# Rebuilding the opening of a linear-attention and MoE kernel: one-bank products for the first 512 tokens, weights cut at column 256, squares redistributed

## The chip, the cores and the metric

One Trainium2 chip, one core. The metric is the device time of one execution in microseconds (us), read on the core. The "clock" of an execution is the mean TensorE clock that its record shows, as a share of full speed.

## The reference, cut to what matters

```python
# q, k, v: [8 batches, 8 heads, 576, 64] f32
q_s = softmax(q, over the 64 dims)
k_s = softmax(k, over the 576 positions)
kv  = einsum('bhsd,bhse->bhde', k_s, v)
x   = einsum('bhsd,bhde->bhse', q_s, kv) -> [4608 tokens, 512]
h   = x @ w_in                       # 512 x 2048
g   = h + sin(alpha * h)**2 / alpha
out = g @ w_out                      # 2048 x 512
```

The 4608 tokens are nine tiles of 512. A batch has 576 tokens, so tile 0 is all of batch 0 but its last 64 tokens. The 2048 hidden columns are 16 "units" of 128. A unit of a tile is four first-layer products, a sine on ScalarE, a square on one of three engines, and a combine (`g`) on VectorE, which frees the unit's PSUM buffer. Then 64 second-layer products follow.

## The kernel before

```python
def load_win(c0, c1):                       # first-layer weights, f32 -> bf16 on the way
    n = slice(c0 * 512, c1 * 512)
    for x in range(2):                      # two halves of the partitions
        nc.gpsimd.dma_start(out=win[64 * x:64 * x + 64, :, n], in_=win_v[x][:, :, n])
...
# opening: batch 0
warm_up(14)                                 # dummy products
norm_q(0, [GP, V])
for c0, c1 in ((0, 1), (1, 2), (2, 4)):     # columns 0-511, 512-1023, 1024-2047
    load_win(c0, c1)
for c in range(3):
    load_wout(c)
cast_v0(0, ACT_CP); cast_v0(1, DVE_CP)
q_transpose(0, 0, ps_s, ACT_CP); q_transpose(0, 1, ps_s, DVE_CP)
cast_v0(2, DVE_CP)
for ii in range(2):
    kv_mm(0, ii, ps_s, split=True); kv_norm(0, ii, ii + 1)
for ii in range(2):                         # all 576 tokens, two-bank products
    attn_out(0, ii, 0, ps_s, (ACT_CP, DVE_CP)[ii])
    attn_out(0, ii, 1, ps_s, (ACT_CP, DVE_CP)[ii])
    warm_up((1, 4)[ii])
...
# tile 0: which engine squares which unit (P GpSimd, A ScalarE, D VectorE)
late = {3: ("q", q, 1, True), 6: ("k", k, 1, False), 8: ("v", v, 1, True)}
for ni in range(nN):
    h_slot(0, ni, "PAPDPAPADPAPPDAP"[ni], lag, lent)
    flush(lag, 1)
    if ni in late:
        ...                                 # loads of batch 1, issued by GpSimd
    if ni == 11:
        load_wout(3)
...
cast_v(1, [GP, GP])
accs = [ps_h.tile([128, dm], F32, name="hp", tag="h") for _ in range(4)]   # of the 4 buffers of ps_h
os = o_quad(0, accs, ...)                   # the 64 second-layer products of tile 0
```

`load_wout` issues a quarter of the second-layer weights, also from GpSimd. The issues: each occupies GpSimd's queue for 0.64 to 0.83 us, and its squares stand in that queue too.

The softmax here doesn't subtract the row's maximum and nothing guards it: scores larger than these inputs give would overflow.

## Time and profile before

| | before |
|---|---|
| median of 3 executions | 296.62 us (296.46 to 296.97) |
| span of the profiled execution | 294.8 us |
| first product of tile 0 | 17.64 us |
| second-layer products before the wait for the accumulators | 9 |
| TensorE resumes after that wait | 34.12 us |
| first product of tile 1 | 49.75 us |

The timelines that carry the argument are in the prediction below. A line of a timeline gives the start and the length of a run of like instructions, then engine, line, operation, "output<-input" and the count; in brackets how long the engine was idle just before, and who ended that. Two more lines of before: the clock row of the page (tenths of full speed in 40 slices), and, from TensorE's timeline, the first product that needs batch 2's q, which a DMA transposes.

```profile
PEclk9999999999999999999999999999999999999999
```

```profile
78.62 0.38 PE L198 MATMUL xp<-qT,kbd 128*128 128x256 bf16 x2 [1.06 <-DMA qT<-qn]
```

### The profile page before, as it was taken

Reading aid. Unit: us, or ns where it says so; the run is one execution under the profiler, and the core shown is the slowest. Engines: PE = TensorE matmul, PEld = TensorE weight load, DVE = VectorE, ACT = ScalarE, POOL = GpSimd, SP = SyncE. Lnnn points to the kernel's source line nnn. Section 1 sums busy time; section 2 is a strip of 40 time slices with the busy share of each in tenths; the row PEclk is TensorE's granted clock in tenths of the full one; section 3 lists DMA queues with packets and bytes.
Section 4 is the critical chain, followed back from the end, with each engine's and each line's share of the span. In section 5 each row is a group of like instructions: output and inputs, shape, how many; then the busy total and the mean of one; then the engine's idle time right before and its main releaser. Section 6 shows DMA issues by size and latency. Waiting matters only on the chain.

```text
span 294.8 us, 4250 instructions
## 1 busy us (share of the span) xinstructions
PE 279.5 (95%) x1576; PEld 132.4 (45%) x1576; DVE 185.9 (63%) x270; ACT 228.1 (77%) x320; POOL 84.6 (29%) x73
## 2 busy tenths in 40 slices
PE   2999999999799999999999999999999999999994
PEld 1544445444344444444444444444444444444443
DVE  3758955789638857865687568756875455555421
ACT  4679855999578899879987999799977777777500
POOL 0939590575665536000700061005000000000000
PEclk9999999999999999999999999999999999999999
DMA  7999989955859986108921794112411111111143
GB/s 261 281 191 207 366 234 364 390 189 165 183 85 323 392 282 139 28 21 290 330 50 36 235 337 98 36 39 60 91 38 36 36 36 38 36 36 37 46 99 72
DMA packets 35221, 45.77 MB, mean 155 GB/s; under 512 B 15856, under 2 KB 19712, under 8 KB 35200
## 3 DMA queue, kind: packets, MB, share of 16 engines
q1 hardware_dynamic: 29600, 34.09, 40.6%
q0 software_dynamic: 5408, 11.27, 14.9%
q8 instruction: 12, 0.20, 0.3%
q10 hardware_dynamic: 192, 0.14, 0.2%
q14 instruction: 9, 0.07, 0.1%
HBM read 36.71 MB, written 9.44 MB: 157 GB/s over the span
## 4 chain that ended last, share of the span: by engine, by line
PE 75%; DVE 9%; ACT 5%; POOL 3%; DMA 3%; issue 2%; ACTq 0%; SPq 0%
PE op L235 31%; PE hp L215 30%; PE hp L235 4%; DVE g L231 3%; PE xp L198 3%; PE warm L279 2%; POOL s L225 2%; DVE xT L201 2%; ACT s L221 2%; PE kvp L154 2%; DMA qT<-qn 2%; DMA st_q<-in_q_dram 1%; DVE o L241 1%; ACT xT L201 1%; PE op L468 1%
## 5 line engine op out<-in xcount | busy, mean ns | idle before, releaser
L231 DVE SCALAR_TENSOR_TENSOR g<-s,inva_sb,hp 128x512 bf16<-128x512 f32 x130 | 95.3, 746 | 65.1 <-ACT s L223 52.3
L215 PE MATMUL hp<-xT,win 128*128 128x512 bf16 x520 | 129.7, 379 | 0.3
L235 PE MATMUL op<-wout,g 128*128 128x512 bf16 x496 | 123.8, 379 | 0.0
L221 ACT ACTIVATE s<-hp,alpha_sb 128x512 f32<-128x512 f32 x130 | 87.8, 682 | 27.0 <-PE hp L215 23.0
L215 PEld LDWEIGHTS <-win 128*128 128x128 bf16 x576 | 56.1, 98 | 68.3 <-issue 2.3
L235 PEld LDWEIGHTS <-g 128*128 128x128 bf16 x560 | 54.0, 98 | 61.9 <-issue 1.0
L223 ACT ACTIVATE s<-s 128x512 f32<-128x512 f32 x112 | 70.5, 629 | 3.6
L144 POOL TENSOR_TENSOR qn<-qe,qs 128x2304 bf16<-128x2304 bf16 (+1 forms) x8 | 26.6, 3328 | 85.2 <-DVE qs L143 79.5
L225 POOL TENSOR_TENSOR s<-s 128x512 f32<-128x512 f32 x27 | 28.4, 1058 | 25.9 <-ACT s L221 25.7
L241 DVE COPY o<-op 128x512 f32<-128x512 f32 (+1 forms) x33 | 21.9, 663 | 14.2 <-PE op L235 11.8
L142 DVE TENSOR_REDUCE qs<-qe 128x18 f32<-128x1152 bf16 (+1 forms) x11 | 20.7, 1880 | 13.1 <-ACT qe L114 13.0
L114 ACT ACTIVATE qe<-st_q 128x1152 bf16<-128x1152 f32 x16 | 17.8, 1155 | 2.8 <-DMA st_q<-in_q_dram 2.7
L114 ACT ACTIVATE ke<-st_k 128x1152 bf16<-128x1152 f32 x16 | 17.7, 1150 | 2.5 <-DMA st_k<-in_k_dram 2.5
L128 POOL CAST vb<-st_v 128x1152 bf16<-128x1152 f32 x14 | 16.5, 1210 | 7.9 <-DMA st_v<-in_v_dram 7.9
L201 DVE CAST xT<-xp 128x512 bf16<-128x512 f32 (+1 forms) x22 | 16.5, 753 | 2.8 <-PE xp L198 2.7
L198 PE MATMUL xp<-qT,kbd 128*128 128x256 bf16 (+1 forms) x64 | 12.4, 285 | 4.2 <-ACT xT L201 1.8
L235 PE MATMUL hp<-wout,g 128*128 128x512 bf16 x64 | 15.1, 379 | 0.4 <-DVE g L231 0.3
L198 PEld LDWEIGHTS <-kbd 128*128 128x128 bf16 x64 | 6.0, 97 | 12.9 <-issue 5.7
L201 ACT CAST xT<-xp 128x512 bf16<-128x512 f32 (+1 forms) x10 | 6.3, 638 | 7.0 <-PE xp L198 6.9
L279 PE MATMUL warm<-qe,identb 128*128 128x512 bf16 x19 | 7.5, 562 | 2.8 <-ACT qe L114 2.8
L154 PE MATMUL kvp<-vb,ke 64*128 64x130 bf16 x288 | 9.8, 216 | 0.4 <-ACT qT L183 0.3
L114 ACT ACT_TABLE_LOAD x7 | 9.0, 1283 | 1.3 <-PEq L484 1.2
(51 smaller groups left out, 112.2 us busy)
## 6 DMA issues: line engine op xcount, KB each, us to landing
out_dram<-o SPq DMA_DIRECT2D x70, 128.0 KB, 2.4
st_q<-in_q_dram SPq DMA_DIRECT2D x5, 1152.0 KB, 6.3
st_k<-in_k_dram SPq DMA_DIRECT2D x5, 1152.0 KB, 8.7
st_v<-in_v_dram SPq DMA_DIRECT2D x5, 1152.0 KB, 10.7
st_k<-in_k_dram POOLq DMA_DIRECT2D x2, 1152.0 KB, 10.8
wout<-in_moe_w_out_dram POOLq DMA_DIRECT2D x4, 512.0 KB, 14.4
st_q<-in_q_dram SPq DMA_DIRECT2D x2, 576.0 KB, 4.6
st_k<-in_k_dram SPq DMA_DIRECT2D x2, 576.0 KB, 6.6
```

The costliest lines, as they stand in the source:

```text
L114: nc.scalar.activation(dst[:, :, ii * 128:(ii + 1) * 128].rearrange("p j (x d) -> p x j d", x=2), src[:, ii::2], AX.Exp)
L142: nc.vector.tensor_reduce(part, src, axis=AXL.X, op=ALU.add)
L144: engs[h].tensor_tensor(dst, src, part.unsqueeze(3).to_broadcast([128, J, w, D]), op=ALU.mult)
L198: nc.tensor.matmul(xp[:, e, 0:n], kt[:, e, ii], qT[:, j0:j1, ii, e * 64:(e + 1) * 64], start=True, stop=True)
L201: eng(xT[:, 2 * ii:2 * ii + 2, c0:c0 + n], xp[:, :, 0:n])
L215: nc.tensor.matmul(hp, win[:, ki, ni * 128:(ni + 1) * 128], xT[:, ki, t * MF:(t + 1) * MF], start=(ki == 0), stop=(ki == 3))
L221: nc.scalar.activation(s, hp, AX.Sin, scale=alpha_sb[:, ni:ni + 1])
L223: nc.scalar.activation(s, s, AX.Square)
L225: nc.gpsimd.tensor_tensor(s, s, s, op=ALU.mult)
L231: nc.vector.scalar_tensor_tensor(G[t][:, ni], in0=s, scalar=inva_sb[:, ni:ni + 1], in1=hp, op0=ALU.mult, op1=ALU.add)
L235: nc.tensor.matmul(acc, G[t][:, ni, j * 128:(j + 1) * 128], wout[:, ni, :], start=(ni == 0), stop=(ni == nN - 1))
L241: eng(o[:, cols], acc)
```

## The change

The intent: give tile 0 its 512 tokens sooner. Batch 0's attention makes four one-bank chunks of 512 tokens (the other 64 tokens follow later), tile 0's first two units start on half of the model dims, and the warm-ups (dummy products) fall from 19 to 10. With this came three things: the first weights are cut at columns 256 and 1024, with the fourth transfer issued after a cast of v on GpSimd; the string of squares and the places of GpSimd's issues are new; batch 1's v is cast by ScalarE and VectorE. The normalised q and its transpose also exchange two axes, through the whole run.

```diff
-    def load_win(c0, c1):
-        n = slice(c0 * 512, c1 * 512)
-        for x in range(2):
+    def load_win(c0, c1, xs):
+        n = slice(c0, c1)
+        for x in xs:
... (qn and qT: axis ii moved ahead of j; copies of qT split in two)
-        warm_up(14)
+    warm_up(9)
-        for c0, c1 in ((0, 1), (1, 2), (2, 4)):
-            load_win(c0, c1)
-        for c in range(3):
-            load_wout(c)
+    load_win(0, 256, (0,))
+    load_win(0, 256, (1,))
+    load_win(256, 1024, (0,))
... (transposes of q in parts)
-        cast_v0(2, DVE_CP)
+    cast_v0(2, GP_CP)
+    load_win(256, 1024, (1,))
+    load_win(1024, 2048, (0, 1))
+    for c in range(2):
+        load_wout(c)
...
+    for c in range(4):
+        xp = ps_h.tile([128, MF], F32, name="hp", tag="h")
+        attn_chunk(0, c, 0, 8, xp)
+        (ACT_CP, DVE_CP)[c % 2](xT[:, c, 0:MF], xp)
...
-        late = {3: ("q", q, 1, True), 6: ("k", k, 1, False), 8: ("v", v, 1, True)}
+        late = {3: ("q", q, 1, True), 7: ("k", k, 1, False), 9: ("v", v, 1, True)}
+        for ni in range(2):
+            mm_h(0, ni, lent, 0, 2)
-            h_slot(0, ni, "PAPDPAPADPAPPDAP"[ni], lag, lent)
+            h_slot(0, ni, "DAPPAPPDPAPPDPAP"[ni], lag, lent)
-            if ni == 11:
-                load_wout(3)
+            if ni in (5, 12):
+                load_wout(2 if ni == 5 else 3)
-        cast_v(1, [GP, GP])
+        cast_v(1, [ACT_CP, DVE_CP])
... (the 64 tokens left over: four small products and one copy among the second-layer products)
```

## The prediction

> **What bounds the kernel now.** I read the first page (busy shares, then the chain by line), then each engine's timeline of the first 50 us, because the change ends there: later it only reorders the axes of the normalised q and its transpose, and splits some instructions.
>
> ```profile
> PE 279.5 (95%) x1576; PEld 132.4 (45%) x1576; DVE 185.9 (63%) x270; ACT 228.1 (77%) x320; POOL 84.6 (29%) x73
> ...
> PE 75%; DVE 9%; ACT 5%; POOL 3%; DMA 3%; issue 2%; ACTq 0%; SPq 0%
> ```
>
> TensorE is busy for 95% and carries 75% of the chain that ends last. Only an opening that lets its dense work start earlier, and keeps it dense, can win. TensorE's timeline from there:
>
> ```profile
> 6.07 6.13 PE L279 MATMUL warm<-qe,identb 128*128 128x512 bf16 x14 [2.82 <-ACT qe L114]
> 12.00 1.22 PE L182 MATMUL tp<-identb,qn 128*128 128x128 bf16 x18
> 13.15 1.46 PE L154 MATMUL kvp<-vb,ke 64*128 64x130 bf16 x36
> ...
> 17.64 1.89 PE L215 MATMUL hp<-xT,win 128*128 128x512 bf16 x8
> ...
> 29.74 1.89 PE L215 MATMUL hh<-xT,win 128*128 128x512 bf16 x8
> 31.47 2.38 PE L235 MATMUL hp<-wout,g 128*128 128x512 bf16 x9
> 34.12 7.71 PE L235 MATMUL hp<-wout,g 128*128 128x512 bf16 x35 [0.28 <-DVE g L231]
> 41.68 0.83 PE L182 MATMUL tp<-identb,qn 128*128 128x128 bf16 x12
> ...
> 44.04 1.20 PE L154 MATMUL kvp<-vb,ke 64*128 64x130 bf16 x36 [0.33 <-ACT qT L183]
> ...
> 49.75 0.59 PE L215 MATMUL hp<-xT,win 128*128 128x512 bf16 x2
> ```
>
> The first real products start at 17.64 us. Tile 0's 64 of them last to 31.47: 13.83 us, 216 ns each, no gap. Nine products of the second layer follow and there is a short wait (0.28 us) for VectorE's result; at 44.04 another (0.33 us) for ScalarE's copy of q transposed. So tile 0 has almost no slack in TensorE: 2 us won at 17.64 would be a full 2 us, if the others keep up. GpSimd's timeline says that they may not:
>
> ```profile
> 19.48 1.03 POOL L225 TENSOR_TENSOR s<-s 128x512 f32<-128x512 f32 x1 [3.43 <-ACT s L221]
> 21.57 1.04 POOL L225 TENSOR_TENSOR s<-s 128x512 f32<-128x512 f32 x1 [1.06 <-ACT s L221]
> 22.55 1.49 POOL L91 DMA_DIRECT2D st_q<-in_q_dram  x2
> 24.05 2.06 POOL L225 TENSOR_TENSOR s<-s 128x512 f32<-128x512 f32 x2
> 26.03 0.80 POOL L93 DMA_DIRECT2D st_k<-in_k_dram  x1
> 26.82 1.42 POOL L91 DMA_DIRECT2D st_v<-in_v_dram  x2
> 28.25 2.15 POOL L225 TENSOR_TENSOR s<-s 128x512 f32<-128x512 f32 x2
> 30.34 0.79 POOL L107 DMA_DIRECT2D wout<-in_moe_w_out_dram  x1
> 31.14 1.05 POOL L225 TENSOR_TENSOR s<-s 128x512 f32<-128x512 f32 x1
> 32.84 1.04 POOL L225 TENSOR_TENSOR s<-s 128x512 f32<-128x512 f32 x1 [0.65 <-ACT s L221]
> ```
>
> From 21.57 to 32.19 GpSimd has no gap: squares of 1.04 us and DMA issues of 0.7 to 0.8 us stand in one queue. It is 29% busy over the run, but in tile 0 it is a second bound.
>
> **What the Trainium skill says.** "DMA: Bandwidth & Descriptors", section "SWDGE vs HWDGE vs iDMA": a DMA that casts can only be issued by GpSimd, which computes its descriptors in software. The trace agrees: each issue occupies GpSimd for 0.64 to 0.83 us. Same page, "Why small descriptors are slow (HBM only)": each packet has a fixed cost. From the DMA view, 705 packets of 0.98 KB (written size) in 14 to 18 us, at a busy share of 1.12 on 16 engines, are 102 ns each; 476 of 1.79 KB in 18 to 22 us, at 1.14, are 153 ns. That is about 40 ns plus 63 ns per KB: it agrees. "TensorE: Matmul & The Clock Gate", part 1: cold products of 512 columns take 427 ns and warm ones 216. Here the 14 warm-ups take 438 ns each, the later products 216, though the clock row reads full: it agrees. "ScalarE: Activation LUTs", "What ACT_TABLE_LOAD costs": 1.283 us; the trace has 1.28.
>
> **The change, part by part: the opening.** Loads of q, k, v are untouched: ScalarE's exponentials still end at 10.54, v's first half lands at 10.90, its last piece about 12.5 (issued near 4.2, 8.3 to land). Warm-ups fall from 14 to 9 (-2.2 us of TensorE), so the transposes of half 0 go right after GpSimd's q (ends 9.99), those of half 1 after VectorE's (11.21), and are done about 12.3 instead of 13.2. ScalarE casts v to 12.07, so k-v products run 12.3 to 13.1 for half 0; GpSimd casts the last piece (512 columns, about 0.55) to 13.05; half 1 ends near 13.7. VectorE normalises, 0.18 + 0.59 each with small gaps: 13.1 to 13.9 and 13.9 to 14.7 (before 14.06 to 15.70). The four chunks are then evacuated alternately: ScalarE 14.35 to 14.95, VectorE 14.75 to 15.45, ScalarE 15.1 to 15.7, VectorE to 16.1. The split groups let products start on the first two chunks, so I place the first at about 15.5 instead of 17.64: 2.1 us. ScalarE loads its sine table to 17.0, first sine at about 17.2 instead of 18.71: 1.5 us.
>
> **The weights' arrival.** In before, columns 0 to 511 of the first weights land at 14.5 and 15.6, columns 512 to 1023 at about 18.4 and 19.1. Now 0 to 255 come first, then 256 to 1023 as one transfer per half. By the packet line, 512 packets of 0.5 KB take 512 x 72 / 16 = 2.3 us and 512 of 1.5 KB 512 x 135 / 16 = 4.3 us; 1024 packets of 1 KB, as now, 1024 x 103 / 16 = 6.6. So the first 1024 columns are complete when they are now, 18.5 to 19.3. Units 0 and 1 can run early (8 products, done by 17.2), but unit 2 needs column 256 and so waits to some 18.7. In before unit 2 started at 19.37. What is left of 2.1 us on TensorE is 0.7 (0 to 1.2).
>
> **The squares.** The string of before gives GpSimd 8 squares and 4.5 us of issues, and one square is done by 20.5. The new one gives it units 2, 3, 5, 6, 8, 10, 11, 13, 15: nine, none early, and a third block of second-layer weights is now issued inside the stage. The sum is 9 x 1.04 + 1.49 + 0.79 + 0.80 + 1.43 + 0.79 = 14.7 us. It can't start before unit 2's sine. If the weights were no limit, that ends at 17.2 + 0.65 + 0.65 + 0.63 (the square of unit 1 on ScalarE) + 0.65 = 19.8; with them at 18.7, 18.7 + 0.86 + 0.2 + 0.65 = 20.4. So GpSimd ends at 34.5 to 35.1, against 33.88 now. Unit 13's square ends 1.04 before, its combine 0.7 later: 34.1 to 34.8. The fourth accumulator takes that unit's PSUM slot, so TensorE resumes dense work there, against 34.12 now. The first two accumulators wait likewise for units 10 and 11 (about 32.5 to 33; now 31.4), so 8 products are done by then, not 9: 0.2 more. Stage result: +0.3 to +1.0.
>
> **Batch 1.** Its v cast moves from GpSimd (2.9 us, done 42.6) to ScalarE and VectorE. v lands at 39.6 and 40.7 whatever the order, since DMA is full until then and the bytes ahead are the same; the casts end about 41.6. But the k-v products at 44.04 wait for ScalarE's copy of the transposed q, not for v, so this saves nothing unless TensorE arrives earlier. Four small products for the 64 tokens left over add 0.15 us, two copies of 768 for one of 1536 about 0.1. Sum: +0.5 to +1.3, middle +0.9. After this TensorE's stages shift as a whole.
>
> **Rivals.** (1) The gain carries through: GpSimd is not what releases the accumulators, or the weights land by 17.5. That the squares were shifted towards GpSimd speaks for it: whoever retuned them should have seen room there. Products start 2.1 us earlier, v's casts allow it at 41.6 instead of 44.04: 294.5 to 295.5. Against it is the gapless queue above. (2) Weights late: small packets run worse than my line, or the cast between the issues leaves a hole. Unit 2 starts at 19.5 to 20, everything moves by a further 0.8: 298.5 to 299. (3) Fewer warm-ups leave TensorE cold: tile 0's first products at 427 ns, up to 1.5 us. Against it: TensorE stays busy from 6.07 to 13.7, and those first products have slack before unit 2. About nothing.
>
> **Range and chances.** The working alone says 297.5. I give rival 1 about a third, because a retuned string suggests a measured benefit that I can't see, and pull the number to 297.0. Range 294.4 to 298.9: rival 1 in full is its low end, rival 2 the high. Two per cent is 5.9 us; the whole span ahead of the first product changes by 2.1, so beyond 2% either way is very unlikely: faster 0.02, same 0.965, slower 0.015.
>
> **What would show it.** First product near 15.5; a hole in TensorE of 1 to 2 us ahead of unit 2, ended by the weights' DMA; GpSimd gapless from about 20.4 to 35; second-layer products starting near 32.5 and resuming after 34.1, VectorE named as releaser; k-v products of batch 1 at 44.5 to 45.3, after ScalarE's copy; tile 1's first product at 50.2 to 51. I am wrong if GpSimd's queue ends before 33 or tile 1 starts before 49.

## The result, and the profile after

The median of four executions is 300.60 us (300.16 to 301.24), of before in the same rounds 296.76 (296.46 to 296.97): a ratio of 1.0132, 95% interval 1.0109 to 1.0155. That is within 2%, but above the predicted range of 294.4 to 298.9. Ratios here are the mean time of one kernel's fast runs over that of the other's fast runs of the same rounds, so not quite the ratio of the medians.

The page after: TensorE's share fell, DMA's share of the chain rose from 3% to 7%, and two slices of the clock row read 8.

```profile
PE 278.6 (93%) x1567; PEld 131.3 (44%) x1567; DVE 186.4 (62%) x272; ACT 228.6 (76%) x322; POOL 84.8 (28%) x78
...
PEclk9988999999999999999999999999999999999999
...
PE 72%; DVE 8%; DMA 7%; POOL 4%; ACT 4%; issue 2%; SPq 1%; ACTq 0%
```

TensorE's timeline after, to be held against the one in the prediction:

```profile
14.28 0.40 PE L154 MATMUL kvp<-vb,ke 64*128 64x130 bf16 x8 [0.71 <-POOL vb L307]
...
16.03 1.95 PE L234 MATMUL hp<-xT,win 128*128 128x512 bf16 x8
21.26 3.26 PE L234 MATMUL hh<-xT,win 128*128 128x512 bf16 x8 [3.28 <-DMA win<-in_moe_w_in_dram]
24.36 3.62 PE L234 MATMUL hp<-xT,win 128*128 128x512 bf16 x16
...
36.28 0.38 PE L254 MATMUL hp<-wout,g 128*128 128x512 bf16 x1 [0.58 <-DVE g L250]
37.71 4.26 PE L254 MATMUL hp<-wout,g 128*128 128x512 bf16 x19 [1.05 <-DVE g L250]
...
49.51 1.20 PE L154 MATMUL kvp<-vb,ke 64*128 64x130 bf16 x36 [0.38 <-DVE qT L187]
...
55.22 3.62 PE L234 MATMUL hp<-xT,win 128*128 128x512 bf16 x16
...
83.42 0.38 PE L206 MATMUL xp<-qT,kbd 128*128 128x256 bf16 x2 [0.39 <-DMA qT<-qn]
```

The first eight products start at 16.03, 1.6 us earlier than before. Then TensorE stands for 3.28 us until the weights of columns 256 to 1023 land. The next eight products (units 2 and 3) last from 21.26 to 24.36, 3.10 us, where eight at 216 ns are 1.73. In the second layer one product, not nine, is done before the accumulators stop it, and tile 1 starts at 55.22 instead of 49.75. (The first eight products go by turns to accumulators 1 and 2, so the second product already needs accumulator 2. An accumulator takes the PSUM buffer of one of the units 10 to 13 and is free when that unit is combined.)

The windows view of TensorE shows why those eight were slow. Columns: stretch in us, its length, TensorE busy (instructions), granted clock, DMA share, GB/s.

```profile
20.50:21.00 0.50, 0.00 (x0) 0.66 1.12 185
21.00:21.50 0.50, 0.24 (x1) 0.50 0.99 147
...
24.00:24.50 0.50, 0.50 (x3) 0.93 1.14 190
```

The clock stands at 0.50 from 20.66 to 24.07 (0.66 and 0.93 are averages over half a microsecond, in which it changes): TensorE ran at half speed just as the weights came.

GpSimd's timeline after:

```profile
13.61 0.62 POOL L307 CAST vb<-st_v 128x512 bf16<-128x512 f32 x1 [1.68 <-DMA st_v<-in_v_dram]
14.17 1.85 POOL L104 DMA_DIRECT2D win<-in_moe_w_in_dram  x3
...
23.93 1.03 POOL L244 TENSOR_TENSOR s<-s 128x512 f32<-128x512 f32 x1 [6.41 <-ACT s L240]
...
34.40 2.04 POOL L244 TENSOR_TENSOR s<-s 128x512 f32<-128x512 f32 x2
...
38.52 1.04 POOL L244 TENSOR_TENSOR s<-s 128x512 f32<-128x512 f32 x1 [0.28 <-ACT s L240]
```

The queue of squares and issues now begins at 23.93 (before: a square at 19.48, and gapless from 21.57) and ends at 39.56 (before 33.88). What hands it on to TensorE is VectorE, in whose timeline after one reads:

```profile
35.48 0.75 DVE L250 SCALAR_TENSOR_TENSOR g<-s,inva_sb,hp 128x512 bf16<-128x512 f32 x1 [1.06 <-POOL s L244]
36.15 0.85 DVE L246 TENSOR_TENSOR s<-s 128x512 f32<-128x512 f32 x1
36.92 2.09 DVE L250 SCALAR_TENSOR_TENSOR g<-s,inva_sb,hp 128x512 bf16<-128x512 f32 x3
```

VectorE waited 1.06 us for unit 10's square from GpSimd. Its combine let one second-layer product go (36.28). Then VectorE's own square of unit 12 ran ahead of unit 11's combine, and only after that combine could TensorE go on (37.71). GpSimd's square of unit 11 had itself ended only at 36.44 (the pair from 34.40), and the combine began at 37.00: so of this last wait VectorE's square explains some 0.6 us, and the rest is GpSimd's queue.

Last, the chain of waits of after, in order of time (start, length, what):

```profile
4.15 9.40 DMA st_v<-in_v_dram
...
14.17 6.95 DMA win<-in_moe_w_in_dram
```

It runs from v's last piece through GpSimd's cast of it to the fourth transfer of weights, which that cast holds back. This suggests that the hold for v is the cause. The experiments tested it: taking the hold away gave no steady gain.

### The profile page after: what moved, and what is told of

It is laid out like the page before. It is cut to its first block, busy times and chain, and to the rows that moved or that the text cites. A ratio compares the mean times of both kernels' runs of the same rounds, so it can differ in the third digit from the quotient of the medians.

```text
span 299.1 us, 4239 instructions
## 1 busy us (share of the span) xinstructions
PE 278.6 (93%) x1567; PEld 131.3 (44%) x1567; DVE 186.4 (62%) x272; ACT 228.6 (76%) x322; POOL 84.8 (28%) x78
## 3 DMA queue, kind: packets, MB, share of 16 engines
q0 software_dynamic: 5408, 11.27, 15.2%
## 4 chain that ended last, share of the span: by engine, by line
PE 72%; DVE 8%; DMA 7%; POOL 4%; ACT 4%; issue 2%; SPq 1%; ACTq 0%
PE op L254 30%; PE hp L234 29%; PE hp L254 4%; DMA st_v<-in_v_dram 3%; POOL s L244 2%; DMA win<-in_moe_w_in_dram 2%; PE hh L234 2%; DVE g L250 2%; PE xp L206 2%; DVE xT L209 2%; PE kvp L154 2%; ACT s L240 2%; DMA qT<-qn 2%; DVE o L260 1%; PE op L506 1%
## 5 line engine op out<-in xcount | busy, mean ns | idle before, releaser
L143 POOL TENSOR_TENSOR qn<-qe,qs 128x1152 bf16<-128x1152 bf16 x13 | 27.4, 2127 | 85.1 <-DVE qs L137 68.3
L244 POOL TENSOR_TENSOR s<-s 128x512 f32<-128x512 f32 x28 | 29.9, 1074 | 30.3 <-ACT s L240 30.1
L136 DVE TENSOR_REDUCE qs<-qe 128x36 f32<-128x2304 bf16 x5 | 12.8, 2553 | 10.7 <-ACT qe L114 10.7
L209 DVE CAST xT<-xp 128x512 bf16<-128x512 f32 (+1 forms) x20 | 15.0, 752 | 2.1 <-PE xp L206 2.0
L128 POOL CAST vb<-st_v 128x1152 bf16<-128x1152 f32 x12 | 13.6, 1162 | 6.8 <-DMA st_v<-in_v_dram 6.8
L206 PE MATMUL xp<-qT,kbd 128*128 128x256 bf16 (+1 forms) x56 | 11.1, 285 | 3.1 <-ACT xT L209 1.6
L234 PE MATMUL hh<-xT,win 128*128 128x512 bf16 x40 | 10.8, 420 | 3.3 <-DMA win<-in_moe_w_in_dram 3.3
L240 ACT ACTIVATE s<-hh,alpha_sb 128x512 f32<-128x512 f32 x10 | 6.9, 687 | 5.9 <-PE hh L234 4.7
L154 PEld LDWEIGHTS <-ke 64*128 64x128 bf16 x288 | 8.3, 93 | 5.0 <-issue 4.4
L250 DVE SCALAR_TENSOR_TENSOR g<-s,inva_sb,hh 128x512 bf16<-128x512 f32 x10 | 7.1, 742 | 5.2 <-POOL s L244 5.2
```

Source lines behind the costliest of these rows:

```text
L143: engs[ii % len(engs)].tensor_tensor(qn[:, ii].rearrange("p j (x d) -> p j x d", x=2), qe[:, ii], part.unsqueeze(3).to_broadcast([128, J, ...
L154: nc.tensor.matmul(kvp[:, e, ii * 130:(ii + 1) * 130], ke[r, j, ii * 128:(ii + 1) * 128], vt[r, j, ii * 130:(ii + 1) * 130], start=(j == 0 ...
L206: nc.tensor.matmul(xp[:, e, 0:n], kt[:, e, ii], qT[:, ii, j0:j1, e * 64:(e + 1) * 64], start=True, stop=True)
L209: eng(xT[:, 2 * ii:2 * ii + 2, c0:c0 + n], xp[:, :, 0:n])
L234: nc.tensor.matmul(hp, win[:, ki, ni * 128:(ni + 1) * 128], xT[:, ki, t * MF:(t + 1) * MF], start=(ki == 0), stop=(ki == 3))
L240: nc.scalar.activation(s, hp, AX.Sin, scale=alpha_sb[:, ni:ni + 1])
```

## The experiments

Eighteen runs were made, all with correct results. The table gathers them: the ratio to before in the same rounds, then, from each run's one profiled execution, the start of unit 2, the number of second-layer products before the wait, the time at which TensorE resumed, and the start of tile 1. The clocks are those of all executions of that run. The profiled execution of before was one of its faster ones (296.58; over all sessions 296.2 to 298.1).

| run | ratio [95%] | unit 2 | products | resumed | tile 1 | clocks |
|---|---|---|---|---|---|---|
| before | 1 | 19.37 | 9 | 34.12 | 49.75 | 0.996 to 1.000 |
| after, first result | 1.0132 [1.0109, 1.0155] | 21.26 | 1 | 37.71 | 55.22 | 0.992 to 0.994 |
| a_again | 1.0063 [1.0003, 1.0122] | 20.80 | 1 | 38.24 | 55.75 | 0.989 to 1.000 |
| a2_again | 1.0060 [1.0040, 1.0079] | 20.45 | 1 | 36.63 | 54.15 | 0.994 to 1.000 |
| e1_dve_cast | 1.0030 [0.9998, 1.0061] | 19.68 | 1 | 34.90 | 52.41 | 0.997 to 1.000 |
| e1_again | 1.0081 [1.0061, 1.0102] | 20.51 | 1 | 36.70 | 54.21 | 0.994 to 0.998 |
| e2_fill | 1.0045 [1.0025, 1.0064] | 20.40 | 1 | 35.10 | 52.61 | 0.998 to 1.000 |
| e9_fill10 | 1.0052 [1.0028, 1.0076] | 19.64 | 1 | 34.88 | 52.39 | 0.998 to 1.000 |
| e3_old_squares | 0.9994 [0.9961, 1.0027] | 19.67 | 9 | 36.10 | 51.88 | 0.994 to 1.000 |
| e4_split | 1.0001 [0.9965, 1.0037] | 17.49 | 1 | 33.57 | 51.08 | 0.994 to 1.000 |
| e5_split_cast | 1.0008 [0.9970, 1.0045] | 17.67 | 1 | 33.44 | 50.95 | 0.993 to 1.000 |
| e6_split_cast_old | 0.9938 [0.9913, 0.9963] | 17.62 | 9 | 33.92 | 49.70 | 0.998 to 1.000 |
| e6_again | 0.9958 [0.9939, 0.9977] | 17.61 | 9 | 33.91 | 49.91 | 0.994 to 1.000 |
| e11_best_cut | 0.9971 [0.9954, 0.9989] | 17.24 | 9 | 32.42 | 49.60 | 0.997 to 1.000 |
| e7_v1_pool | 1.0043 [1.0005, 1.0081] | 20.48 | 1 | 36.67 | 54.18 | 0.993 to 1.000 |
| g2_best_v1_pool | 0.9970 [0.9950, 0.9991] | 17.17 | 9 | 33.80 | 49.59 | 0.992 to 1.000 |
| f1_before_cut | 1.0021 [0.9997, 1.0044] | 19.88 | 9 | 34.63 | 50.25 | 0.997 to 1.000 |
| f2_before_string | 1.0058 [1.0037, 1.0079] | 18.96 | 1 | 34.57 | 51.92 | 0.998 to 1.000 |
| g1_before_v1 | 0.9947 [0.9930, 0.9963] | 18.75 | 9 | 34.14 | 49.76 | 0.998 to 1.000 |

f1, f2, g1 and e8_axes_before start from the kernel before, all others from the kernel after. e8 is not in the table: 0.9978 [0.9964, 0.9993].

**First set: one suspect each.** The theory was that the fourth transfer of weights is late because GpSimd holds it for v, and that this gap and the half clock after it are the loss. The rivals were GpSimd's sum of squares and issues, and the cut of the weights itself.

e1_dve_cast gives the held cast to VectorE, so that the issue of weights doesn't wait:

```diff
-    cast_v0(2, GP_CP)
+    cast_v0(2, DVE_CP)
```

> The changed kernel with one edit: the last piece of batch 0's v is cast on VectorE, so GpSimd no longer waits for that piece between the third and the fourth issue of first-layer weights. Theory 1 (the wait for v holds back the weights' issue): the fourth issue moves from 14.17 to about 12 us, the weights of unit 2 land near 19.2 instead of 21.1, the gap of TensorE shrinks to under 1.5 us, its clock stays warm, and the time falls by 2.5 to 3.5 us to 297 to 298. Rival (the DMA engines are full and the landing is set by bytes and packets, not by the issue): unit 2 still starts at 20.8 or later and the time stays within 0.7 us of 300.6.

Measured: 297.94 us, 1.0030. Unit 2 started at 19.68 after a gap of 1.86 us, and the clock stayed full. By itself this looks like most of the first result's loss (1.0132) found. It did not hold up, see e1_again.

e2_fill keeps TensorE busy in the gap, with 14 dummy products into unit 2's own accumulator, which the real ones then overwrite:

```diff
             hp = wide()
+            if t == 0 and ni == 2:
+                for _ in range(14):
+                    nc.tensor.matmul(hp, identb, A["qe", 0][:, 0:4, 0:128], start=True, stop=True)
```

> The changed kernel with 14 products without use (identity times batch 0's exponentials) put into unit 2's accumulator ahead of its real ones, so TensorE is busy while it waits for the weights. Theory: unit 2 still starts at 21.2, but its 8 first products take 216 ns, not 427, so 1.7 us are won in tile 0 and, with GpSimd's chain starting 0.7 to 1.2 us earlier, the time falls by 1 to 1.5 us to 299.1 to 299.6. Rival (the cold clock is hidden behind GpSimd's chain): less than 0.4 us.

Measured: 298.31 us, 1.0045. No execution had a clock under 0.998. But the fill itself ended at 20.40, while the weights had landed at about 18.95: it was too long, and the run is inconclusive on the clock's worth.

e3_old_squares takes back the string and the places of the issues, and nothing else:

```diff
-    for c in range(2):
+    for c in range(3):
         load_wout(c)
-        late = {3: ("q", q, 1, True), 7: ("k", k, 1, False), 9: ("v", v, 1, True)}
+        late = {3: ("q", q, 1, True), 6: ("k", k, 1, False), 8: ("v", v, 1, True)}
-            h_slot(0, ni, "DAPPAPPDPAPPDPAP"[ni], lag, lent)
+            h_slot(0, ni, "PAPDPAPADPAPPDAP"[ni], lag, lent)
-            if ni in (5, 12):
-                load_wout(2 if ni == 5 else 3)
+            if ni == 11:
+                load_wout(3)
```

> The changed kernel with the string of squares, the moments of batch 1's loads and the issues of the second-layer weights as before (8 squares and 4.5 us of issues on GpSimd instead of 9 and 5.3, unit 0's square before the gap). The weights and the cold clock stay as they are. Theory: after a late unit 2 GpSimd's sum is the bound, so 1.5 to 2.2 us are won: about 298.5 to 299.1; GpSimd's last square of tile 0 ends near 37.0 instead of 39.6. Rival (the stage is set by the late weights and TensorE alone): no gain, within 0.5 us of 300.6.

Measured: 297.09 us, 0.9994: parity with before. TensorE's timeline of this run:

```profile
33.44 2.38 PE L254 MATMUL hp<-wout,g 128*128 128x512 bf16 x9
```

Nine products run without a wait, as before, although unit 2 came at 19.67 after a gap of 2.04 us and the clock stood at half until 23.62. So the string is worth about 0.6% in this opening, held against the two repeats of after below (1.006).

e4_split keeps the new string and the held cast, and takes back only the cut of the weights:

```diff
-    load_win(0, 256, (0,))
-    load_win(0, 256, (1,))
-    load_win(256, 1024, (0,))
+    load_win(0, 512, (0,))
+    load_win(0, 512, (1,))
+    load_win(512, 1024, (0,))
...
-    load_win(256, 1024, (1,))
+    load_win(512, 1024, (1,))
```

> The changed kernel with the column cuts of the first-layer weights as before (512, 512, 1024 instead of 256, 768, 1024); order of issue, the wait for v and everything else stay. Units 2 and 3 then need only the first transfer, and the late one is met by unit 4. Theory: the gap before unit 2 goes (or is under 0.5 us, if the first 512 columns land after 17.9), a gap of under 2 us is left before unit 4, TensorE stays warm, and the time falls by 3 to 4 us, to 296.5 to 297.5. Rival (the cut costs nothing, only the sum of bytes counts): unit 4 waits until 21 or later with the clock cold, and the gain is under 1.5 us.

Measured: 296.68 us, 1.0001: parity too, again 0.6% under the repeats of after. TensorE's timeline of this run:

```profile
17.49 1.89 PE L234 MATMUL hh<-xT,win 128*128 128x512 bf16 x8
...
33.57 4.26 PE L254 MATMUL hp<-wout,g 128*128 128x512 bf16 x19 [1.05 <-DVE g L250]
```

Unit 2 starts with no gap, and only later, ahead of unit 8 at 24.13, does TensorE wait 1.29 us for weights. The wait of 1.05 us for VectorE's combine is the same as in after, only 4.1 us earlier: it belongs to the string, its place in time to the weights.

**Second set: do they add, and is anything else in it?** Beside them the kernel after was run again, unedited.

> The changed kernel once more, unedited, on the chip of the runs beside it. The weights of unit 2 landed at 21.1 us in its first profile, but unit 2 started at 19.7 in the run with the old squares, whose opening is the same. Theory 1 (the hold for v costs 1.5 us of landing, always): unit 2 at 20.8 or later here too, and 300 to 301.2 us. Rival (the landing scatters by more than a microsecond from run to run or chip to chip, and the first profile was a late one): unit 2 at 19.5 to 20.5 and a time of 298.5 to 300.

Measured: 298.70 us, 1.0063, half the first result's loss. The first result's chip is not on record, so a trait of that chip stays a possible reason for the other half. The four executions fall apart by clock: 297.76 and 297.73 at 1.000 and 0.998; 299.64 at 0.991 and 301.43 at 0.989. In the profiled one (the 301.43) the clock was at half for 6.83 us, from 19.94 to 26.77.

e5_split_cast is e4's cut with e1's cast:

> The changed kernel with the column cuts as before and the last piece of v cast on VectorE, so no hold in the weights' issue; the new string of squares stays. Theory: TensorE runs tile 0 without a gap from about 15.9 us (unit 4's weights land by 19.2), and what remains is GpSimd's sum of 14.7 us from unit 2's sine at about 19.6: it ends near 34.4, as with the split alone (35.4 there), and the time is 296.2 to 297.0. Rival (the weights were the whole cost): 294.5 to 295.5, since the first product is 1.7 us earlier than before.

Measured: 297.51 us, 1.0008. The cast adds nothing to the cut.

e6_split_cast_old is e5 with e3's old string:

> As the run with the cuts and the cast on VectorE, and the string of squares, the loads and the weights' issues as before too. What is left of the change is the one-bank products, the split first groups, the fewer warm-ups, the new axes and batch 1's cast. Theory: TensorE is dense from 15.9 us, GpSimd ends near 33.0, dense second-layer work resumes near 33, one us ahead of before, and the time is 295.3 to 296.2, the first clear gain. Rival (batch 1's chain gives it back: its keys and values land where they did): 296.4 to 297.2.

Measured: 295.43 us, 0.9938: faster than before, by the whole interval. Beside e5, on the same chip, the string is 0.7%. Starting from e6, the string (0.0070) and the cut (e3 less e6, 0.0056, though from two chips, and e6 has e1's cast too) add up to 1.0064, where a_again measured 1.0063. So these two add, and explain what after costs on an ordinary day. Why e6 is faster than before was not clear at this point: its tile 1 starts when before's does.

e7_v1_pool gives batch 1's v back to GpSimd:

```diff
-        cast_v(1, [ACT_CP, DVE_CP])
+        cast_v(1, [GP_CP, GP_CP])
```

> The changed kernel with batch 1's v cast back on GpSimd, everything else as changed. Theory: the key-value products of batch 1 wait for the copy of the transposed q (49.4 us in the first profile), and GpSimd's casts end by 48, so nothing changes: within 0.5 us of the changed kernel of this call. Rival (the cast moved because GpSimd would be too late): the products start 1 us later and the time rises by 1 us.

Measured: 299.03 us, 1.0043. The k–v products started at 48.47, 12 us after TensorE had resumed (36.67), as they do in after (49.51 and 37.71): to them the cast makes no difference. I read the run as "no effect", because the ratio is within the scatter of a_again's. Its profile said otherwise: the wait for batch 2's transposed q at 83 us is 1.01 us in it, and 0.39 in after.

**Third set: the hold and the clock once more, and the axes.** a2_again is after once more, e1_again is e1_dve_cast once more, in the same rounds.

> The changed kernel unedited, as the measure for its two neighbours on this chip. Theory: executions fall in two groups by the granted clock: about 297.7 at 0.997 or more, 299.5 to 301.5 at 0.995 or less. Rival: no relation between the clock and the time.

> The changed kernel with the last piece of v cast on VectorE, beside the unedited kernel on one chip, because without it the landing of the weights could not be compared. Theory (the hold for v delays the landing by about a microsecond): unit 2 starts 0.7 to 1.5 us earlier than in the unedited kernel beside it, mostly with the clock kept, and the time is 1 to 2 us lower. Rival (chip and moment decide the landing): the two start within 0.4 us of each other.

Measured: a2_again 298.78 us, 1.0060; e1_again 299.64 us, 1.0081. From GpSimd's and TensorE's timelines of e1_again:

```profile
9.84 3.88 POOL L104 DMA_DIRECT2D win<-in_moe_w_in_dram  x6
```

```profile
20.51 2.46 PE L234 MATMUL hh<-xT,win 128*128 128x512 bf16 x8 [3.06 <-DMA win<-in_moe_w_in_dram]
```

All six issues go out in one piece, the fourth at about 11.8 instead of 13.54 as in a2_again, and still unit 2 starts at 20.51, against 20.45, and the time is no lower (1.0081 beside 1.0060). So taking the hold away gives no steady gain, and my theory of the first set fell here. I first put this down to full transfer engines (DMA share about 1.1 from 18 to 23 us in both runs). The windows view says otherwise for the time before: first e1_again, then e1_dve_cast, the same kernel.

```profile
14.00:14.50 0.50, 0.28 (x2) 1.00 0.66 12
14.50:15.00 0.50, 0.33 (x2) 1.00 0.17 18
```

```profile
14.00:14.50 0.50, 0.28 (x8) 1.00 0.97 139
14.50:15.00 0.50, 0.41 (x2) 1.00 0.84 123
```

All six transfers had been issued by 13.7, yet in e1_again next to nothing was moved from 14 to 15 us (12 and 18 GB/s), where its twin moved 139 and 123 GB/s and started unit 2 at 19.68. Why the traffic stalled is open. That the chain of waits of after runs through the cast of v is true as a record of what released what, and no proof of a cause.

e9_fill10 is e2_fill with 10 dummies, so that the fill ends before the weights land.

> The changed kernel with 10 products without use, not 14, ahead of unit 2: they end near 19.5 us, before or just when the weights land, and leave TensorE idle for less than 2 us. Theory (what lifts the changed kernel from 297.7 to above 299.5 in some executions is the fall of TensorE's clock in the gap): all executions have a clock of 0.997 or more, agree within 0.8 us, and lie at 297.3 to 298.2. Rival (the clock record goes along with a late landing and is not the cause): a scatter of more than 1.5 us as in the unedited kernel.

Measured: 298.38 us, 1.0052, with no clock under 0.998 and only 0.33 us of wait left ahead of unit 2. Yet its executions go from 297.70 to 299.75, no less scattered than a2_again's 298.19 to 299.76. So keeping the clock up takes away neither the loss nor the scatter. In a2_again the two executions with a clock of 0.994 were 1.1 us slower in the mean than the other three, in a_again the two slow ones 2.8 us. A fallen clock goes with a late landing, and the data doesn't part the two cleanly.

e8_axes_before puts only the new axes of q and its transpose into before (5 rounds). I wanted to know whether they give the shorter wait at 83 us.

> The kernel before with the new axes of the normalised q and its transpose alone (half first, then row block), and the copies split by half. In the changed kernel and in its best mixture 0.7 us come back near 78 us: the transfer that transposes batch 2's q lands 4.6 to 4.7 us after its issue, where before it took 5.4, and TensorE's wait for it falls from 1.06 to 0.4 us. Theory (the new axes make that transfer quicker): it lands in 4.7 us here too, the wait is about 0.4 us, and the time falls by 0.4 to 0.9 us against before. Rival (other traffic made it slow in that one profile): no difference beyond 0.3 us.

Measured: 296.48 us, 0.9978 [0.9964, 0.9993]. The wait at 79 us is 1.02 us, so the axes alone don't shorten it: the mechanism that I expected is refuted, though the kernel is 0.2% faster. Its tile 1 starts at 50.36, 0.6 us late, but from the start of the last copy to the end of the span it takes 3.7 us, where before takes 4.2. The profile doesn't say why.

**Fourth set: each cause alone in the opening of before, and a better version.**

f1_before_cut:

```diff
-        for c0, c1 in ((0, 1), (1, 2), (2, 4)):
+        for c0, c1 in ((0, 0.5), (0.5, 2), (2, 4)):
```

> The kernel before with one edit: the first-layer weights are cut at columns 256 and 1024 instead of 512 and 1024. Theory (the cut makes units 2 and 3 wait for all of the first 1024 columns, which land at 19.5 to 21): unit 2 starts at 19.7 to 21 instead of 19.4, GpSimd's queue shifts by the same, and the time rises by 0.3 to 1.3 us. Rival (the cut only hurts together with the early start of unit 0): no change, within 0.3 us.

Measured: 297.14 us, 1.0021 [0.9997, 1.0044]. Unit 2 waits 1.31 us and starts at 19.88 (before 19.37), and tile 1 is 0.5 us late. In the old opening, where the first product comes late anyway, the cut costs little, and it isn't clear that it costs anything.

f2_before_string is before with e3's edit reversed: new string, new places of the issues.

> The kernel before with the new string of squares, the new moments of batch 1's loads and of the second-layer weights' issues, and nothing else. Theory (nine squares and 5.3 us of issues, none before unit 2, are too much for GpSimd): its last square of tile 0 ends near 36.2 instead of 33.9, the unit-13 combine near 36, dense second-layer work resumes about 1.9 us later with 8 products fewer done, and the time rises by 1.5 to 2.5 us. Rival (the string is only bad after a late unit 2): less than 0.5 us.

Measured: 298.56 us, 1.0058 [1.0037, 1.0079], all clocks at 0.998 or more. From its TensorE and GpSimd timelines:

```profile
34.57 9.44 PE L235 MATMUL hp<-wout,g 128*128 128x512 bf16 x43 [1.05 <-DVE g L231]
```

```profile
35.38 1.04 POOL L225 TENSOR_TENSOR s<-s 128x512 f32<-128x512 f32 x1 [0.28 <-ACT s L221]
```

The same wait of 1.05 us after a single product, with no wait ahead of unit 2 and no fallen clock. (Unit 8 waits 0.87 us for weights, but GpSimd has no gap from 21.18 to 35.09, so that isn't what holds it up.) GpSimd ends at 36.42, against 33.88 in before. The string alone makes as large a loss as the whole change does on an ordinary day: it is the part that was wrong by itself.

e11_best_cut is e6 with the last 1024 columns cut in two, to take away the wait of 1.31 us that e6 has ahead of unit 8:

```diff
-    load_win(1024, 2048, (0, 1))
+    load_win(1024, 1536, (0, 1))
+    load_win(1536, 2048, (0, 1))
```

> The mixture that beat before (new opening, old cuts, old string, v's last piece cast on VectorE) with the last 1024 columns of the weights cut into two of 512. In the mixture unit 8 waited 1.3 us for the last 1024 columns (24.4 us). Theory: unit 8 starts near 22.9, GpSimd then sets the end, and 0.3 to 0.8 us more are won: 294.7 to 295.2. Rival (smaller packets and two more issues eat it): no gain over the mixture, within 0.3 us.

> The mixture once more, as measure for the run beside it and on whatever chip this is. Theory: 1.0 to 2.0 us below before (ratio 0.993 to 0.997), every execution with the clock kept. Rival (it won by the chance of one chip): ratio 0.998 or more.

Measured: e11_best_cut 296.03 us, 0.9971; e6_again 295.57 us, 0.9958. The wait ahead of unit 8 is gone, and TensorE resumes at 32.42, 1.5 us earlier than e6 (after a first stop of 0.31 us behind eight products). Then, in e11's TensorE timeline:

```profile
42.59 0.50 PE L185 MATMUL tp<-identb,qn 128*128 128x128 bf16 x6 [1.24 <-DVE xT L399]
```

VectorE's copy of the 64 left-over tokens stands in its queue behind the cast of batch 1's v, which hasn't landed, and TensorE waits 1.24 us for it. Tile 1 starts at 49.60, only 0.3 us before e6's 49.91, and the wait for the transposed q is back at 1.02 us. The gain is given back by the next limit: the arrival of batch 1.

**Fifth set: the cast of batch 1's v by itself.** e6 beats before by 0.6 and 0.4% on two chips, with the same start of tile 1. Its gain comes later: 0.7 us at the wait for the transposed q (0.37 instead of 1.06) and 0.5 us after the last copy. With e7 in mind, g1_before_v1 puts nothing but the cast into before, and g2_best_v1_pool takes nothing but the cast out of e6:

```diff
 g1, from before:
-        cast_v(1, [GP, GP])
+        cast_v(1, [ACT_CP, DVE_CP])
 g2, from e6:
-        cast_v(1, [ACT_CP, DVE_CP])
+        cast_v(1, [GP_CP, GP_CP])
```

> Before, with batch 1's v cast by ScalarE and VectorE instead of GpSimd, nothing else. Theory: this part of the change gives the shorter landing of batch 2's transposed q (e7, which takes it back, shows a wait of 1.01 us there, after 0.39). Then the wait at about 78.6 us falls from 1.06 to about 0.4 and the time by about 0.65 us, ratio 0.998. Rival: the landing of 4.7 or 5.4 us is a matter of when other transfers stand in the queues (e11 has the cast moved and waits 1.02 all the same); then this run may show either, and the cast alone explains nothing.

> The best version so far (new opening, old cut, old string, v's last piece on VectorE), with batch 1's v cast back on GpSimd. Theory: the wait for batch 2's transposed q is about 1.0 us again instead of 0.36, the rest is unchanged: some 0.65 us slower than the best version, ratio 0.997 to 0.998. Rival, timing of other transfers decides: the wait may stay near 0.4 and the ratio near 0.995.

Measured: g1 295.66 us, 0.9947 [0.9930, 0.9963], more than twice the gain that I expected; g2 296.14 us, 0.9970, 0.1 to 0.3% above the two runs of e6, with intervals that overlap. From g1's TensorE timeline, then its GpSimd timeline:

```profile
49.76 3.62 PE L215 MATMUL hp<-xT,win 128*128 128x512 bf16 x16
...
77.94 0.38 PE L198 MATMUL xp<-qT,kbd 128*128 128x256 bf16 x2 [0.36 <-DMA qT<-qn]
```

```profile
39.21 0.81 POOL L93 DMA_DIRECT2D st_q<-in_q_dram  x1
```

Tile 1 starts when it does in before, and the wait is 0.36 us instead of 1.06. In g2 it is 1.02. What the cast changes is when GpSimd comes to issue the loads of batch 2: at 39.21 in g1, at 42.54 in before, where GpSimd first waits for v and casts it. Of the thirteen other runs of the table with the cast moved, twelve wait 0.34 to 0.39 us and e11 waits 1.02; those with it on GpSimd (before, e7, e8, f1, f2, g2) wait 1.01 to 1.06. So that the cast moves this landing is shown, from both sides. How is open: e11 issues batch 2's loads at 39.05 and waits all the same. The 0.5 us after the last copy come with the cast (g1) and with the axes (e8) alike, and they stay in e7 and g2, which have the axes and not the cast (3.7 us; before, f1 and f2 take 4.1 to 4.4). They aren't explained.

The best versions are thus e6 (0.9938 and 0.9958) and g1 (0.9947), which can't be told apart. g1 is one line. The new opening itself, freed of its cut, its string and the cast (g2), starts tile 1 0.16 us earlier than before does: next to nothing. Most of its 0.3% is the shorter end.

## Why the prediction was wrong

The number was 297.0, the range 294.4 to 298.9, the result 300.6. The working put the sum at +0.9 us; the profiled span is 4.3 us longer. My estimate of the 3.4 us between, from the times below: late weights 2.6 (step 2), half clock 1.2 (step 3: from unit 2 to resuming it took 16.45 us, and 15.22 in e1_dve_cast at full clock), eight products behind a wait 1.5 (step 5); against that 1.2 won after tile 1 (step 7) and some 0.5, because an earlier unit releases TensorE than I had: 3.6 in all. By the prediction's own steps:

1. **First product at about 15.5: right.** 16.03; 15.2 to 16.0 in the other runs of this opening. But 17.64 was a late start for before: the runs with its opening (f1, f2, g1, e8) start at 16.69 to 17.24, so the gain to be had was nearer 1.4 us than 2.1.

2. **The weights' arrival, unit 2 at 18.7: right in kind, too small.** A hole ahead of unit 2, ended by the weights' DMA, was predicted and is there. But unit 2 started at 21.26 (20.80 and 20.45 in the repeats, 19.67 in e3, whose opening is the same), not at 18.5 to 19.3. This is the largest miss. The term that was mis-sized is the time per packet: I took 72 ns for packets of 0.5 KB and 135 for 1.5 KB, from a line fitted to before. After has 557 packets from 10 to 14 us at a share of 0.76 of 16 engines, which are 88 ns each, and 796 from 14 to 21.3 us at a share of 1.08, which are 159 ns for 1.6 KB, where my line gives 141. v's last piece also came at 13.56, not 12.5. I took the landing as fixed by bytes; in these four profiles it scattered by 1.6 us. What sets that scatter is open.

3. **Rival 3, cold clock, "about nothing": the step that failed.** I looked for cold products only among the first eight and argued with TensorE's work up to 13.7 us. But my own step 2 had a hole in it, and the clock fell near that hole in all six profiles whose hole ahead of unit 2 was 2.04 us or longer, and in none with a shorter one. Units 2 and 3 took 3.10 us instead of 1.73, which is 1.4 us, in the first result, and 2.9 us over units 2 to 7 in a_again. All four executions of the first result had a clock of 0.992 to 0.994. (A mean of 0.997 or 0.998 needs no fall in the opening: in the profiles with such a mean the clock falls only after the last product, in e11 from 292.4 us of 294.1.) Over the thirteen unedited executions the five with 0.997 or more have a mean of 298.18, the eight others one of 300.36. The first kind is inside my range, the second isn't. e9_fill10 says that this 2.2 us is not the clock alone: the late landing that opens the hole is in it too.

4. **GpSimd's sum of 14.7 us from unit 2's sine: right.** 23.93 to 39.56 is 15.6 us; it began 3.5 us later than the 20.4 that I had, of which 2.6 are the weights and 0.8 the half clock (2.67 us from unit 2's first product to this square, 1.83 in e1_dve_cast).

5. **Which accumulator stops TensorE: the other mis-sized term.** I took the fourth, at unit 13's combine, and had units 10 and 11 free the first two at 32.5 to 33, in time for eight products; the lost ninth I gave 0.2 us. Measured: the second accumulator, after one product, at unit 11's combine, which stands behind GpSimd's squares of units 10 and 11 and VectorE's own square of unit 12. The eight products that before does ahead of its wait stand behind it here, 8 x 0.216 = 1.7 us. From resuming to tile 1 it takes 17.5 us in after and 15.6 in before. f2 shows that this holds without a wait ahead of unit 2: resumed at 34.57, inside my 34.1 to 34.8, and tile 1 at 51.92, above my 50.2 to 51. I could have seen the square of unit 12 in the string. It explains about 0.5 us in f2 (unit 11's square ends at 33.30, its combine starts near 33.8); the rest is GpSimd's queue. No run moved that square alone.

6. **Batch 1, "this saves nothing": right for the k–v products, wrong for the kernel.** They waited for a copy of the transposed q, not for v, as predicted. But I asked only who waits for v, not what GpSimd does next: freed of the cast, it issues batch 2's loads 3.3 us earlier. The edit is worth 0.5% in before (g1); that the earlier loads are the path is not shown (e11). It is the largest gain of any part by itself (the axes alone give 0.2%, e8), and I had booked it at zero.

7. **"After this the stages shift as a whole": not quite.** Tile 1 is 5.5 us late and the span only 4.3 us longer. Of the 1.2 us, 0.7 come from the wait for the transposed q (1.06 to 0.39 us) and 0.5 from the end of the span after the last copy. The first goes with the cast of step 6 (e7 and g2 lose it again), the second with the cast or with the axes (g1, e8). g1 gets 1.2 us after tile 1 too. The q of batch 2 lands 4.7 us after its issue instead of 5.4; by what path the earlier loads do that is open.

8. **The choice of the number.** The working said 297.5. I pulled it to 297.0 because a retuned string suggested a benefit that I couldn't see. There was none: f2_before_string shows the string as the largest single loss. The working itself was near what the undisturbed executions gave (298.2), and wrong for the disturbed ones.

So the gain of 1.4 to 2.1 us at the first product was turned into a wait for weights by the cut at column 256, then into half-speed products in most executions, and what was left was lost behind GpSimd's longer queue. In per cent of the time, each from runs of its own: the string +0.6 to +0.7 (f2; e5 against e6), the cut +0.4 to +0.6 in this opening (e3 against the two runs of e6; e4 against the repeats), the rest of the change -0.4 to -0.6 (e6, with e1's cast). The sum is +0.4 to +0.9, against +0.6 measured in the two repeats; the first result's other 0.7 goes with a clock that fell in every execution. In the rest, the cast alone is -0.5 (g1) and the opening with the axes -0.3 (g2); these don't add, as both have the same shorter end of the span. Only argued, not shown, is how much of the scatter between sessions is the clock and how much the landing.

## What to carry to other kernels

An early start is worth nothing if the data of the next step lands when it always did: cut transfers by what each unit reads, and when a prediction has a hole of 2 us or more in TensorE, count half-speed products after it (here 2.04 us was enough, 1.86 was not). Judge a split of work between engines by the order in which buffers come free and by what the relieved engine issues next, not by sums of busy time: three squares put ahead of one combine, two in GpSimd's full queue and one on VectorE, moved eight products behind a wait, and one cast less on GpSimd was the largest gain. And a chain of waits names who released whom; whether that was the cause only an experiment shows that moves it.

## What the Trainium skill lacked or had wrong

- "TensorE: Matmul & The Clock Gate", Part 1, "What's actually happening", has the clock fall to half after at least one idle window of about 3.4 us. In these runs less was enough: a gap of 2.04 us (e3_old_squares, half clock from 20.21 to 23.62), while one of 1.86 us left it full (e1_dve_cast). A gap of 3.06 us that ended at 20.51 made it fall at 21.69, 1.2 us after work had resumed (e1_again). The length agrees with the page: half clock lasted 3.41 us, or twice that (6.83 us in a_again, where the first of the two windows was busy for 2.55 us of 3.41 and didn't bring the clock back). That a window which is only partly idle, or partly busy, counts as idle isn't on the page.
- The same page doesn't say how this shows in a mean clock over an execution: one window at half in 299 us is 1 - 0.5 x 3.41 / 299 = 0.994, and two are 0.989, which are among the values that the slower executions show (0.989 to 0.994; the fall after the last product, in step 3 above, takes up to 0.003 more). The 14 cold warm-ups of before (438 ns each), on the other hand, leave the clock row at full.
- "DMA: Bandwidth & Descriptors", "Why small descriptors are slow (HBM only)", gives the fixed cost of a packet in cycles and metadata bytes, but no time per packet for casting transfers beside others: here 88 ns at 0.5 KB and 159 ns at 1.6 KB. The prediction's "it agrees" holds only in kind: its line has 40 ns per packet. Nor has any page that the same transfer's landing scatters between executions of one kernel: unit 2 started at 20.45, 20.80 and 21.26 us in three profiles of the same instructions.
